# Where the first FFN's raw weights are staged, and how far ahead they are loaded, in an attention and two-FFN kernel

## The chip, the core and the metric

The kernel runs on one core of one Trainium2 chip. The metric is device time in microseconds (us) of one execution. Engines are named as in the profile: PE (TensorE matmul), PEld (its weight loads), DVE (VectorE), ACT (ScalarE), POOL (GpSimd), SP (SyncE, whose queue issues every DMA here).

## What is computed

Attention with a window of 64 positions over q, k and v of shape (4, 8, 576, 64); its output, as 2304 tokens of 512, goes through an FFN with ELU (512 to 2048 to 512), and that through an RMS norm and a gated SiLU FFN (512 to 1536 to 512).

```python
attn = softmax(where(0 <= i - j < 64, q @ k.T / sqrt(D), -1e9)); x = (attn @ v) as (2304, 512)
h = x @ w_in;  x = where(h > 0, h, exp(min(h, 0)) - 1) @ w_out
xn = x / sqrt(mean(x * x) + 1e-6) * rms_g
g = xn @ w_gate;  out = (g * sigmoid(g) * (xn @ w_val)) @ w_out2
```

All weights arrive as 64-bit floats, so the kernel reads them as pairs of 32-bit words and has to make 32-bit floats of them itself.

## The kernel before

**Stages.** The 2304 tokens run in six blocks of 384 through the first FFN (loop at L792). While block b is multiplied, the attention of block b + 1 is worked in between (`att_runs`, L269). The attention of block 0 stands alone ahead of the loop (L776 to L780). Block 0 is special: while it runs, all weights of the first FFN are converted, and they stay in SBUF for the other five blocks. From block 1 on the weights of the second FFN are prepared in the background (`prep_matrix`) and written to DRAM; the second FFN then runs from L853.

**A unit.** The first FFN's weights are 32 units of 512 columns (`w1src`, L743 to L747: in 0, in 1, out 0, in 2, out 1, ...). `Feeder` takes a unit through four stages, one unit behind the other. `load` (L317) gets a place for the 512 KB of raw words and issues the DMA (L326). `s1` takes the magnitude from the high words (ACT L333), turns the low words into their bits in place (ACT L334), clips (L336: DVE for even units, POOL for odd ones) and joins the two (DVE L338). `s2` puts in the sign (DVE L345), after which the raw words are free, gets a place for the finished unit and writes its rounded half there (L353, ACT or DVE as the planner picks). `s3` writes the remainder (POOL L359). Between these the value lies in a `wm` tile, of which there are three. `step` (L363) does `s3` of unit n - 2, `s2` of unit n - 1, `s1` of unit n, and then loads up to unit n + AHEAD - 1; three steps run before block 0 and two per hidden tile in it.

**Places.** Pool `wp` has 32 places of 4 KB per partition under one tag, `wu` (L62). Each of the 32 finished units takes one for good. Before block 0 the attention's tiles use free ones of them (`a_tile`, two half tiles to a place, 15 places in all). `tmp4` (L123) is a place of this pool for raw words or such tiles; `big4` (L293) is one of three buffers of the same size in pool `mp`, which also serve the norm (`norm_items`, L435) and the second FFN's raw words (L755). In the kernel before, raw words with an odd number, and all from 25 on, go to `big4`, the others to `tmp4`.

**Order.** The program is written in Python order, and a planner at compile time puts each engine's instructions in a fixed order from a simulated timeline; it may pull an instruction ahead of older ones that aren't ready in that timeline. Places of a tag are given out in that timeline. On the chip each engine, and SP's queue too, works its list in order: an instruction that waits holds up all behind it. PE multiplies in `mm_in` (L403) and `mm_y` (L430); between them `elu` and `split_g` run on ACT (L421, L422) and DVE (L423, L412, L413). `x_split` (L386, L387, DVE) prepares a block's input.

Of the kernel before, what the change touches and what calls it, by code (L numbers as in the profile page):

```python
# [20 lines left out]
def kernel(  # L21
# [30 lines left out]
    assert sum(BLOCKS1) == NT and H * D == DM  # L52
    PITCH0 = 1
    NSTART = 3
    AHEAD = 4
    PS0 = 12
    AHEAD2 = 6
    NS0 = 2
# [64 lines left out]
    def tmp4():  # L123

        return wp.tile([128, 1024], F32, tag="wu", name="tmp4")
# [167 lines left out]
    def big4():  # L293
        return mp.tile([128, 1024], F32, tag="big4", name="big4", bufs=3)

    def unit():
        return wp.tile([128, 2, 512], F32R, tag="wu", name="wu")

    def w_cols(w, f):

        return w.bitcast(I32)[:, f * 256:(f + 1) * 256].rearrange("(k p) f -> p k f", p=128)
# [311 lines left out]
    def prep_out(j):  # L613

        n, f, d = 4 * NP2 + j, OF[j], {}

        def first():
            fwp.load(n + 1)
            fwp.s1(n)

        def second():
            fwp.load(n + 2)
            d[0] = fwp.sign(n)

        def half(h):
            split_out(ospill[:, f, :].rearrange("p (a c) -> p a c", a=2)
                      [:, :, h * 256:(h + 1) * 256], d[0][:, h * 256:(h + 1) * 256])

        return [first, second, lambda: half(0), lambda: half(1)]
# [113 lines left out]
    w1src = [(("in", 0), w_cols(w_in, 0))]  # L743
# [12 lines left out]
    prep = [fn for t in range(2 * NP2) for fn in prep_matrix(t)]  # L756
    PREP_PER = -(-len(prep) // (len(BLOCKS1) - 2))
    prep_o = [fn for j in range(F2) for fn in prep_out(j)]
    fw1 = Feeder(w1src, lambda: big4() if fw1.loaded % 2 or fw1.loaded > 24 else tmp4(), lambda i: unit(), AHEAD, pool=True)

    n0 = BLOCKS1[0] // 128
    setup()
# [174 lines left out]
```

## Time and profile before

| | |
|---|---|
| median of three executions | 963.12 us (960.55 to 964.42) |
| the profiled execution | 966.99 us, of which the span is 965.2 us |
| PE busy | 920.6 us, 95% of the span |
| PEld busy | 866.8 us, 90% |
| DVE busy | 648.8 us, 67% |
| ACT busy | 491.5 us, 51% |
| POOL busy | 212.4 us, 22% |
| q1, the DMA queue that SP issues to | 181.96 MB, 58.1% of 16 engines' span |

Shares of the whole span are means over stages with different limits: PE is busy in nearly all of the second half, DVE in the first block. So the views below are cut to the stretch from about 20 to 144 us, in which the first FFN's weights are converted.

### The profile page before, as it was taken

The numbers are of one execution on the slowest core, as the hardware profiler recorded it, in microseconds if no ns is written. First come the engines' busy times: TensorE is split into PE (matmuls) and PEld (weight loads), VectorE is DVE, ScalarE is ACT, GpSimd is POOL, SyncE is SP. The second block draws the span as 40 slices with busy tenths as digits, with TensorE's granted clock in tenths as the row PEclk, the third lists the DMA queues.
The fourth block names the chain that finished last, engine by engine and source line by source line (L and its number), as shares of the span: only waits on it lengthen the run. The fifth ranks groups of instructions, "written<-read, shape, count | busy, mean of one in ns | idle before, by whom it ended". The sixth has DMA issues, their size and how long they took to land.

```text
span 965.2 us, 16463 instructions
## 1 busy us (share of the span) xinstructions
PE 920.6 (95%) x5916; PEld 866.8 (90%) x5916; DVE 648.8 (67%) x1449; ACT 491.5 (51%) x1201; POOL 212.4 (22%) x228
## 2 busy tenths in 40 slices
PE   6588989999999999999999999999999999999998
PEld 5487989988899899998999999899998998998996
DVE  2899998758776877776788588178363276561471
ACT  5787766665576566556545456344141442341440
POOL 2465650245245114404402100200000000000000
PEclk9699889999999999999999999999999999999999
DMA  9556530765565266546438729791984747945721
GB/s 230 165 164 193 145 110 22 203 207 162 152 197 160 92 186 187 153 107 194 162 118 276 250 69 386 278 354 48 401 327 144 280 123 246 374 136 210 235 72 66
DMA packets 150402, 183.02 MB, mean 190 GB/s; under 512 B 81712, under 2 KB 111408, under 8 KB 150320
## 3 DMA queue, kind: packets, MB, share of 16 engines
q1 hardware_dynamic: 150320, 181.96, 58.1%
q8 instruction: 47, 0.77, 0.3%
q14 instruction: 35, 0.29, 0.1%
HBM read 144.18 MB, written 37.75 MB: 188 GB/s over the span
## 4 chain that ended last, share of the span: by engine, by line
PE 63%; DVE 12%; DMA 8%; ACT 7%; POOL 4%; issue 3%; SPq 0%; POOLq 0%; DVEq 0%; ACTq 0%
PE y L691 16%; PE w L691 12%; PE y L725 10%; PE w L403 9%; PE y L430 9%; DMA pspill<-stg 5%; PE w L725 5%; DVE wm L338 3%; POOL stg L562 3%; ACT s L207 2%; DVE wm L345 2%; DVE g L412 1%; DMA big<-in_moe_w_gate_dram 1%; DVE wm L336 1%; DVE e L423 1%
## 5 line engine op out<-in xcount | busy, mean ns | idle before, releaser
L403 PE MATMUL w<-x,wu 128*128 128x384 f32 x1152 | 228.2, 346 | 17.2 <-DVE e L423 9.5
L430 PE MATMUL y<-g,wu 128*128 128x384 f32 x1152 | 223.3, 340 | 3.7 <-DVE g L412 2.5
L403 PEld LDWEIGHTS w<-x,wu 128*128 128x128 f32 x1152 | 205.7, 193 | 23.4 <-DVE e L423 11.2
L430 PEld LDWEIGHTS y<-g,wu 128*128 128x128 f32 x1152 | 201.2, 189 | 8.3 <-DVE g L412 3.9
L691 PE MATMUL y<-xw,pu 128*128 128x384 f32 x864 | 161.6, 334 | 0.0
L691 PEld LDWEIGHTS y<-xw,pu 128*128 128x128 f32 x864 | 151.2, 188 | 0.8
L562 POOL TENSOR_TENSOR stg<-wm,stg 128x256 fp32r<-128x256 f32 x72 | 64.8, 906 | 293.2 <-ACT stg L561 285.3
L691 PE MATMUL w<-xw,pu 128*128 128x384 f32 x648 | 123.7, 334 | 0.0
L657 DVE TENSOR_TENSOR c<-c,w 128x384 f32<-128x384 f32 x72 | 39.7, 551 | 118.5 <-PE w L691 117.6
L691 PEld LDWEIGHTS w<-xw,pu 128*128 128x128 f32 x648 | 113.3, 188 | 0.3
L725 PE MATMUL y<-wu,g 128*128 128x512 f32 x432 | 106.4, 390 | 0.0
L725 PEld LDWEIGHTS y<-wu,g 128*128 128x128 f32 x432 | 80.9, 188 | 16.2
L423 DVE SCALAR_TENSOR_TENSOR e<-e,w 128x384 f32<-128x384 f32 x96 | 52.5, 548 | 55.2 <-ACT e L422 54.9
L421 ACT ACTIVATE e<-w 128x384 f32<-128x384 f32 x96 | 46.3, 483 | 55.3 <-PE w L403 55.3
L653 ACT COPY c<-y 128x384 f32<-128x384 f32 x72 | 34.3, 480 | 67.9 <-PE y L691 67.3
L413 DVE TENSOR_TENSOR g<-e,g 128x384 fp32r<-128x384 f32 x96 | 62.5, 652 | 1.6
L725 PE MATMUL w<-wu,g 128*128 128x512 f32 x216 | 55.9, 390 | 0.0
L359 POOL TENSOR_TENSOR wu<-wm,wu 128x512 fp32r<-128x512 f32 x32 | 45.8, 1441 | 41.7 <-ACT wu L353 27.3
L673 ACT CAST g<-e 128x384 fp32r<-128x384 f32 x69 | 34.7, 511 | 37.2 <-DVE e L667 37.2
L207 ACT ACTIVATE s<-s,st 128x128 f32<-128x128 f32 x120 | 46.6, 390 | 10.7 <-DVE st L203 10.7
L662 ACT ACTIVATE e<-c 128x384 f32<-128x384 f32 x54 | 27.5, 524 | 47.2 <-DVE c L657 47.2
L422 ACT ACTIVATE e<-e 128x384 f32<-128x384 f32 x96 | 50.1, 524 | 1.8
(126 smaller groups left out, 1209.5 us busy)
## 6 DMA issues: line engine op xcount, KB each, us to landing
pu<-pspill SPq DMA_DIRECT2D x126, 512.0 KB, 6.5
pspill<-stg SPq DMA_DIRECT2D x84, 256.0 KB, 2.2
wu<-ospill SPq DMA_DIRECT2D x36, 512.0 KB, 5.3
big<-in_moe_w_out_dram SPq DMA_DIRECT2D x16, 512.0 KB, 4.9
big<-in_moe_w_in_dram SPq DMA_DIRECT2D x15, 512.0 KB, 3.9
vw<-in_v_dram SPq DMA_DIRECT2D x27, 256.0 KB, 3.7
tmp<-in_moe_w_out_dram SPq DMA_DIRECT2D x12, 512.0 KB, 4.7
big<-in_moe_w_gate_dram SPq DMA_DIRECT2D x12, 512.0 KB, 5.1
```

Of the source, the lines that this page charges most:

```text
L207: nc.scalar.activation(out=s[:, p, :], in_=s[:, p, :], func=AF.Exp, scale=-1.0, bias=st[:, 0, p, :], accum_out=st[:, 1, p, :])
L359: eng.tensor_tensor(out=u[:, 1, :], in0=m, in1=u[:, 0, :].bitcast(F32), op=ALU.subtract)
L403: nc.tensor.matmul(pt[:, :n], lhsT=wt[:, a, kk * 128:(kk + 1) * 128], rhs=xs[kk][:, c, :n], start=(i == 0), stop=(i == len(seq) - 1))
L413: nc.vector.tensor_tensor(out=g[:, 1, :n], in0=src[:, :n], in1=g[:, 0, :n].bitcast(F32), op=ALU.subtract)
L421: nc.scalar.activation(out=e[:, :n], in_=ph[:, :n], func=AF.Relu, scale=-1.0)
L422: nc.scalar.activation(out=e[:, :n], in_=e[:, :n], func=AF.Exp, scale=-1.0)
L423: nc.vector.scalar_tensor_tensor(out=e[:, :n], in0=e[:, :n], scalar=-1.0, in1=ph[:, :n], op0=ALU.add, op1=ALU.max)
L430: nc.tensor.matmul(py[m][:, :n], lhsT=wt[:, a, m * 128:(m + 1) * 128], rhs=g[:, c, :n], start=(first and i == 0), stop=(last and i == 2))
L562: nc.gpsimd.tensor_tensor(out=t[:, 1, :], in0=src, in1=t[:, 0, :].bitcast(F32), op=ALU.subtract)
L657: nc.vector.tensor_tensor(out=t, in0=t, in1=bank[b, qi][:, :NB], op=ALU.add)
L691: nc.tensor.matmul(bank[key][:, :NB], lhsT=u[:, qi, a, kk * 128:(kk + 1) * 128], rhs=X[j][kk][:, x, :], start=(first and n == 0), stop=(n ...
L725: nc.tensor.matmul(po[m], lhsT=g[:, a, (m % 3) * 128:(m % 3 + 1) * 128], rhs=w[:, x, :], start=(first and i == 0), stop=(last and i == 2))
```

## The change

Two lines differ. Every raw unit of the first FFN goes to a place of `wp`, and none to the three `big4` buffers; and a step loads eight units ahead instead of four. At step n there are then n finished units and the raw words of units n to n + 7, at most 24 + 8 = 32 places. Nothing that is computed changes, and no instruction is added or removed.

```diff
-    AHEAD = 4
+    AHEAD = 8
@@
-    fw1 = Feeder(w1src, lambda: big4() if fw1.loaded % 2 or fw1.loaded > 24 else tmp4(), lambda i: unit(), AHEAD, pool=True)
+    fw1 = Feeder(w1src, tmp4, lambda i: unit(), AHEAD, pool=True)
```

## Rows read from the trace of the kernel before

**Rows 1.** Busy time by stretch: start:end, length; PE, PEld, DVE, ACT, POOL; clock, DMA share, GB/s

```profile
22.00:45.00 23.00, 10.71 (x126) 8.78 (x125) 17.59 (x60) 17.99 (x54) 9.72 (x8) 0.72 0.60 165
42.00:76.00 34.00, 28.70 (x197) 27.47 (x198) 33.86 (x68) 25.61 (x59) 20.37 (x14) 0.85 0.58 178
76.00:110.00 34.00, 28.86 (x203) 26.80 (x201) 32.72 (x62) 25.23 (x59) 21.76 (x15) 0.90 0.49 149
110.00:144.00 34.00, 31.07 (x208) 28.81 (x207) 33.59 (x63) 23.08 (x55) 20.49 (x14) 0.90 0.53 139
133.00:965.00 832.00, 817.77 (x5156) 773.86 (x5155) 539.33 (x1195) 395.27 (x959) 141.50 (x161) 1.00 0.57 192
```

**Rows 2.** Chain that ended last, around 133 us: start, length, what

```profile
131.71 1.37 DVE g L412
...
133.13 1.67 PE y L430 x8
```

**Rows 3.** Waits, 38 to 144 us: engine and line, releaser, total, times, longest

```profile
ACT big L334 <- DMA big<-in_moe_w_in_dram: 2.5, 2, 1.6
DVE e L423 <- ACT e L422: 1.1, 1, 1.1
```

**Rows 4.** SP's queue in order of time, 20 to 48 us: start, length, issue

```profile
25.93 1.34 SPq L326 DMA_DIRECT2D big<-in_moe_w_in_dram  x2
27.31 1.36 SPq L326 DMA_DIRECT2D tmp<-in_moe_w_out_dram  x2
42.42 0.38 SPq L326 DMA_DIRECT2D big<-in_moe_w_in_dram  x1
...
47.36 0.61 SPq L119 DMA_DIRECT2D ks<-in_k_dram  x1
```

**Rows 5.** PE in order of time at 74.9 us

```profile
74.93 0.44 PE L164 MATMUL w<-ident,ks 128*128 128x128 f32 x2
```

**Rows 6.** DMA issues, 38 to 130 us: KB each, median us to landing

```profile
tmp<-in_moe_w_out_dram SPq DMA_DIRECT2D x9, 512.0 KB, 4.6
```

**Rows 7.** All engines in order of time, 33.9 to 38.6 us; [idle before, releaser]

```profile
34.20 0.76 DVE L353 CAST wu<-wm 128x512 fp32r<-128x512 f32 x2
34.70 3.87 POOL L359 TENSOR_TENSOR wu<-wm,wu 128x512 fp32r<-128x512 f32 x3 [12.15 <-DVE wu L353]
...
36.13 0.67 ACT L333 ACTIVATE wm<-big 128x512 f32<-128x512 f32 x1
...
37.75 0.67 ACT L333 ACTIVATE wm<-tmp 128x512 f32<-128x512 f32 x1
...
38.45 0.43 DVE L336 TENSOR_SCALAR wm<-wm 128x512 f32<-128x512 f32 x1 [3.50 <-ACT wm L333]
```

**Rows 8.** All engines in order of time at 75.2 us

```profile
75.20 1.31 POOL L359 TENSOR_TENSOR wu<-wm,wu 128x512 fp32r<-128x512 f32 x1 [1.30 <-ACT wu L353]
75.29 1.77 DVE L338 SCALAR_TENSOR_TENSOR wm<-wm,big 128x512 int32<-128x512 int32 x1
```

**Rows 9.** DVE groups by shape, 38 to 144 us: count, busy us, mean ns, idle before

```profile
L338 DVE SCALAR_TENSOR_TENSOR wm<-wm,big 128x512 int32<-128x512 int32 x18 | 18.8, 1051 | 0.0
...
L412 DVE CAST g<-e 128x384 fp32r<-128x384 f32 x15 | 11.7, 779 | 0.1
...
L338 DVE SCALAR_TENSOR_TENSOR wm<-wm,tmp 128x512 int32<-128x512 int32 x11 | 10.5, 959 | 0.2
```

**Rows 10.** Lines L338 and L412 over the whole span: ns min/median/max, first to last start

```profile
L338 DVE SCALAR_TENSOR_TENSOR wm<-wm,big x55: 677/693/1782, 22.6 to 606.0; 128x512 int32<-128x512 int32 x55
...
L412 DVE CAST g<-e x96: 342/360/1445, 57.5 to 548.6; 128x384 fp32r<-128x384 f32 x96
```

**Rows 11.** DVE groups by shape in the stretches 42:76, 76:110 and 110:144

```profile
L338 DVE SCALAR_TENSOR_TENSOR wm<-wm,big 128x512 int32<-128x512 int32 x5 | 5.1, 1026 | 0.0
...
L338 DVE SCALAR_TENSOR_TENSOR wm<-wm,big 128x512 int32<-128x512 int32 x5 | 5.7, 1141 | 0.0
...
L338 DVE SCALAR_TENSOR_TENSOR wm<-wm,big 128x512 int32<-128x512 int32 x8 | 8.7, 1094 | 0.0
```

## The prediction

> **What bounds the kernel now.** I read the table of busy time by stretch first, then the chain that ended last, then the waits of the stretch that the change touches. From 133 us on PE is the bound: it is busy 817.77 of 832 us, so 14.2 us are idle in all that follows [rows 1]. In block 0, where the first FFN's weights are converted, it is DVE: 33.86, 32.72 and 33.59 of 34 us in three equal stretches, while ACT has 8 to 11 us free in each and PE 3 to 5 [rows 1]. The chain says the same: it runs over DVE until 133.1 us and goes over to PE there [rows 2]. So block 0 ends when DVE has done its list, and a microsecond that DVE gains or loses ahead of 133 us moves the end by about one. An earlier load helps only as far as DVE stood still for want of it.
>
> **What the loads cost now.** Waits on a raw load are small: ACT stood still twice for one, 2.5 us in all [rows 3]. DVE stood still once in the stretch, 1.1 us, behind ACT's exponential [rows 3], and 3.50 us just at its start, behind ACT's L333 [rows 7].
>
> **Part 1, every raw unit in the weight pool.** It removes SP's waits for one of three big buffers. Unit 9 was issued at 42.42, far behind the four loads at 25.93 to 28.67 [rows 4]; unit 9's buffer had come free when DVE had put in the sign of unit 3. After the change the loads from 4 on can follow each other from about 26 us. Counting places by the code, there are at most 24 + 8 = 32 of 32: the last raw unit takes the place of unit 23's raw words and finished unit 24 that of its own, which the same DVE instruction frees that the rounding waits for anyway. That costs nothing; the cover is that dependency, and if a place were short the loads alone would wait, with seven units in hand.
>
> **Part 2, eight ahead.** It adds no transfer; it moves about four of 512 KB (some 2.1 MB) forward into 26 to 45 us. The engines there are 60% busy at 165 GB/s [rows 1], so 275 GB/s when busy, 7.6 us for the four, against 23 x 0.4 = 9.2 us free. Queued behind them on SP is the load of the next keys, now at 47.36 [rows 4], which PE reads at 74.93 [rows 5]: 27 us of cover, where a load takes 4.6 us [rows 6]. If that cover were gone, one late load would cost PE up to those 4.6 us. It is not: loads wait for fewer buffers than before. Three buffers lie idle for all of block 0 and are next used by the norm behind it, in the same order as before; nothing is gained there.
>
> **ACT's order.** Since L334 needs only the raw words, the planner can pull it further forward into ACT's gaps. That moves work and adds none: with 25.6 of 34 us busy [rows 1], ACT has room. The 2.5 us of waits go away, but DVE had work while ACT waited (its only idle place was the 1.1 us), so I count at most that 1.1 us.
>
> **The start.** The 3.50 us of DVE are not a load's: unit 0 is rounded at 34.20, POOL then takes three remainders in 3.87 us from 34.70, and ACT's L333 follow at 36.13 and 37.75 as the three `wm` tiles come free [rows 7]. Earlier raw words do not free a `wm` tile. Between nothing and 3.5 us I take nothing, since the rows name POOL's chain.
>
> **What POOL takes from DVE.** This is DVE's one large term that depends on the order. At 75.20 POOL starts L359, to end at 76.51; DVE's L338, started at 75.29, takes 1.77 us and ends 0.55 us behind POOL [rows 8], where the median is 693 ns [rows 10]. Over block 0 the two kinds L338 and L412 alone lose 18 x (1051 - 693) + 11 x (959 - 693) + 15 x (779 - 360) ns = 6.4 + 2.9 + 6.3 = 15.6 us so [rows 9, 10]. Both engines keep all their instructions, but a new order pairs them anew. How much that can be I take from the three stretches, which are three pairings of the same work: L338 on big buffers means 1026, 1141 and 1094 ns [rows 11], a loss of 333, 448 and 401, within 15% of their middle. So 15% of 15.6 us, 2.3 us to either side, with zero as the likeliest.
>
> The Trainium skill (SBUF — State Buffer, "Who interferes with whom") says that VectorE and GpSimd share one pair of ports as an exclusive lock, and that the order of issue decides who blocks. The trace agrees for the pair at 75.2 us. Taken to its end, the rule speaks against reading an unchanged list of instructions as an unchanged time; the rival on pairing below is that case.
>
> **The sum.** The profiled execution took 966.99 us, its span is 965.2, and 1.8 lie around it. Gain 1.1, start 0, pairing 0, blocks 1 to 5 0: 965.9. That execution stands 3.9 us above the median of 963.12; carried to the median it is **962.0 us**, which differs from before by less than the 0.5% (4.8 us) that a measurement of this kernel can tell from no change.
>
> **Rivals.**
> *Faster: the start closes up.* If the loads in hand let the planner fill DVE's 3.50 us (input split or roundings there) besides the 1.1, and pairing falls well, it is 3.5 + 1.1 + 2.3 = 6.9 us: 956 us. For it: DVE stands free there and ACT has gaps to use. Against it: the three `wm` tiles, and the input split that needs the attention's end.
>
> *Slower: the first roundings come behind more loads.* Places of one tag are given out in the program's order. Before, unit 0's place stood ahead of raw unit 4's; now it stands behind raw units 4 to 7, unit 1's behind 8, unit 2's behind 9. If the planner thereby puts the first roundings (34.20) later, the three `wm` tiles stay full longer, L333 at 36.13 and 37.75 and DVE at 38.45 come later by as much [rows 7], and DVE is full from there on. An issue took 0.67 us of SP [rows 4]; six are 4.0 us, with pairing up to 6.3: 969 us. It decides from 4.8 us on. Against it: SP had issued such loads by 28.67, before the place is wanted at 34.20 [rows 4, 7], so the chip need not wait even where the plan does.
>
> *Pairing alone.* If the order on DVE and POOL changed so much that the 15.6 us move by over 30%, the time would leave 958 to 968 on either side, 957 or 969. Three stretches within 15% speak against it.
>
> *The loads do not come earlier.* SP's queue is in order, and a place given out late could hold the raw loads where they are: 963 us. Against it: 32 places, some never used before 42 us.
>
> **How the numbers follow.** Forecast 0.50; start closes up 0.22; first roundings later 0.13; pairing 0.09 (a third each faster, slower and within); loads not earlier 0.06. Faster by over 0.5%: 0.22 + 0.03 = 0.25; slower: 0.13 + 0.03 = 0.16; within: 0.59. The range takes the bounds: 1.1 + 3.5 + 2.3 = 6.9 below 963.1 gives 956.2, 4.0 + 2.3 = 6.3 above gives 969.4; with one more microsecond on each side for the 14.2 us of PE's idle time behind 133 us, which a new order can touch, 955 to 970.5.
>
> **What the profile after would show.** Right: no L326 on SP waits for L345 before the pool is full; units 4 to 9 are issued in one run from about 26 us; no ACT wait on a raw load between 38 and 144; DVE still 96% or more busy there, with the same means of L338 and L412 within 15%; the chain goes over to PE between 131 and 135 us. Start closed: DVE's wait at 38.45 is gone and the handover is before 129. First roundings late: L353 behind 36 us, handover behind 137. What would make the prediction wrong: a handover that moves by over 5 us, or PE's idle time behind it far from 14 us.

## The result, and the profile after

The changed kernel takes 970.19 us (median of five runs, 968.09 to 972.24), the kernel before 963.49 us beside it (960.55 to 964.42): a ratio of 1.0066 with a 95% interval of 1.0048 to 1.0084. It is slower by some 6 us. The forecast was 962.0, no change; 970.19 lies just inside the slow end of the range (955 to 970.5), where the prediction had put late first roundings and pairing.

Busy time by stretch after, for [rows 1]:

```profile
22.00:45.00 23.00, 10.67 (x118) 8.49 (x119) 15.98 (x57) 20.67 (x59) 9.36 (x7) 0.66 0.89 279
42.00:76.00 34.00, 26.81 (x155) 26.06 (x156) 33.14 (x65) 25.37 (x59) 19.47 (x13) 0.80 0.39 127
76.00:110.00 34.00, 27.36 (x194) 25.20 (x193) 33.61 (x62) 24.88 (x59) 20.51 (x13) 0.90 0.57 171
110.00:144.00 34.00, 29.48 (x234) 27.13 (x233) 33.86 (x65) 21.67 (x51) 23.05 (x15) 0.90 0.27 62
133.00:965.00 832.00, 820.58 (x5158) 777.87 (x5159) 539.46 (x1195) 394.41 (x956) 144.09 (x163) 0.99 0.57 190
```

Over the three stretches DVE is as full as before (100.6 and 100.2 us), and PE behind 133 us is no less busy. What has changed is PE ahead of it: 26.81, 27.36 and 29.48 us against 28.70, 28.86 and 31.07. One row over all of block 0 shows it, first of before, then of after:

```profile
43.00:160.00 117.00, 104.62 (x723) 98.53 (x724) 113.12 (x233) 84.89 (x205) 64.30 (x42) 0.90 0.48 140
```

```profile
43.00:160.00 117.00, 99.66 (x699) 93.93 (x700) 109.63 (x212) 78.33 (x182) 64.63 (x42) 0.88 0.40 113
```

PE stood idle 12.4 us there before and 17.3 us after, and had done 24 matmul records less by 160 us. How late PE is can be read at a matmul record of a given number. In the kernel before, 965 records start ahead of the norm of block 0 (L458), the last of them at 160.24 us; in the changed kernel the 965th starts at 164.49, 4.2 us later. PE in order of time, before and after:

```profile
160.24 0.34 PE L430 MATMUL y<-g,wu 128*128 128x384 f32 x1
160.41 0.81 PE L458 MATMUL w<-big,ones 128*128 128x384 f32 x2
```

```profile
164.49 2.24 PE L430 MATMUL y<-g,wu 128*128 128x384 f32 x12
166.57 0.81 PE L458 MATMUL w<-big,ones 128*128 128x384 f32 x2
```

The chains of before and of after show where the time went:

```profile
160.58 0.65 PE w L458 x2
```

```profile
132.24 0.60 DVE s L216
...
133.43 0.75 issue
134.18 1.11 DVE s L216
...
135.42 1.09 PE w L223 x4
136.51 3.11 PE w L403 x12
...
166.73 0.65 PE w L458 x2
```

The norm is 6.2 us later, but 976 records stand ahead of it in PE's new order, 11 more than before, and these take 1.9 us. Of the 4.2 us at the 965th record, 2.3 are there when the chain goes over to PE (135.4 us, 133.1 in [rows 2]), and 2.0 come behind it, where PE has more left to do. DVE puts the sign into the last of the 32 weight units at 144.7 us instead of 143.2, 1.4 later. At the end of the span 5.3 us are lost (965.2, now 970.5), so most of the loss is there when block 0 ends. Behind it the distance at records of the same number is no constant: it lies between 1.8 and 7.0 us in the next three blocks.

Where PE waits, 43 to 166 us (line, releaser, total, times, longest), before and after:

```profile
PE w L403 <- DVE e L423: 5.6, 2, 3.9
PE w L403 <- DVE x L386: 3.3, 1, 3.3
PE w L223 <- ACT wu L353: 1.8, 1, 1.8
PE w L403 <- ACT wu L353: 1.7, 1, 1.7
...
PE w L223 <- DVE s L216: 0.6, 1, 0.6
```

```profile
PE w L403 <- DVE e L423: 6.8, 2, 4.7
PE w L403 <- DVE x L386: 5.8, 1, 5.8
PE w L223 <- DVE st L215: 5.8, 2, 3.2
PE w L223 <- DVE s L216: 2.2, 2, 1.3
PE y L430 <- DVE g L412: 1.1, 1, 1.1
```

With the small ones left out here, the waits are 15.2 us before and 21.7 after (e12 below has 20.0 and is hardly late, so this sum is no measure of the delay). The largest new one is the transposes of the next block's attention (L223), which stand in PE's queue ahead of FFN matmuls and wait for the scaling of the softmax (L214 to L216) on DVE: 0.6 us before, 8.0 after.

The loads did what the change says. SP's queue from 25 us, first and last of one run of ten raw units:

```profile
25.50 1.05 SPq L326 DMA_DIRECT2D tmp<-in_moe_w_out_dram  x1
...
33.68 0.38 SPq L326 DMA_DIRECT2D tmp<-in_moe_w_in_dram  x1
```

279 GB/s instead of 165 in that stretch, and no wait of ACT on a raw load is left between 38 and 144 us. What else is new is the order in which the planner put the work. The list of instructions is the same; 11 copies that may go to either engine changed between ACT and DVE (by the lists that e1 and e2 below hold), and on DVE, ACT, PE and POOL the sequence is another one almost from the beginning.

### The profile page after: what moved, and what is told of

The parts are those of the page before. It is cut to its first block, busy times and chain, and to the rows that moved or that the text cites. A ratio compares the mean times of both kernels' runs of the same rounds, so it can differ in the third digit from the quotient of the medians.

```text
span 970.5 us, 16477 instructions
## 1 busy us (share of the span) xinstructions
PE 917.6 (95%) x5916; PEld 865.1 (89%) x5916; DVE 649.4 (67%) x1450; ACT 491.3 (51%) x1200; POOL 213.0 (22%) x228
## 4 chain that ended last, share of the span: by engine, by line
PE 65%; DVE 10%; DMA 7%; ACT 7%; POOL 5%; issue 3%; SPq 2%; POOLq 0%; DVEq 0%; ACTq 0%
PE y L691 15%; PE w L691 12%; PE y L725 10%; PE w L403 10%; PE y L430 10%; PE w L725 5%; DMA pspill<-stg 5%; POOL stg L562 3%; DVE wm L338 3%; DVE wm L345 2%; ACT s L207 2%; SPq L119 1%; DMA big<-in_moe_w_val_dram 1%; ACT wm L333 1%; POOL sw L591 1%
## 5 line engine op out<-in xcount | busy, mean ns | idle before, releaser
L403 PE MATMUL w<-x,wu 128*128 128x384 f32 x1152 | 226.3, 345 | 16.6 <-DVE e L423 10.3
L430 PE MATMUL y<-g,wu 128*128 128x384 f32 x1152 | 223.1, 340 | 4.5 <-ACT kT L178 2.3
L403 PEld LDWEIGHTS w<-x,wu 128*128 128x128 f32 x1152 | 206.6, 194 | 20.5 <-DVE e L423 12.2
L430 PEld LDWEIGHTS y<-g,wu 128*128 128x128 f32 x1152 | 200.9, 189 | 9.2 <-issue 4.3
L691 PE MATMUL y<-xw,pu 128*128 128x384 f32 x864 | 161.6, 334 | 0.0
L423 DVE SCALAR_TENSOR_TENSOR e<-e,w 128x384 f32<-128x384 f32 x96 | 52.6, 547 | 49.7 <-ACT e L422 49.2
L413 DVE TENSOR_TENSOR g<-e,g 128x384 fp32r<-128x384 f32 x96 | 61.7, 644 | 1.8
L359 POOL TENSOR_TENSOR wu<-wm,wu 128x512 fp32r<-128x512 f32 x32 | 45.8, 1440 | 46.3 <-ACT wu L353 42.0
L422 ACT ACTIVATE e<-e 128x384 f32<-128x384 f32 x96 | 50.4, 525 | 1.9
```

What stands on the lines that cost most here:

```text
L359: eng.tensor_tensor(out=u[:, 1, :], in0=m, in1=u[:, 0, :].bitcast(F32), op=ALU.subtract)
L403: nc.tensor.matmul(pt[:, :n], lhsT=wt[:, a, kk * 128:(kk + 1) * 128], rhs=xs[kk][:, c, :n], start=(i == 0), stop=(i == len(seq) - 1))
L413: nc.vector.tensor_tensor(out=g[:, 1, :n], in0=src[:, :n], in1=g[:, 0, :n].bitcast(F32), op=ALU.subtract)
L422: nc.scalar.activation(out=e[:, :n], in_=e[:, :n], func=AF.Exp, scale=-1.0)
L423: nc.vector.scalar_tensor_tensor(out=e[:, :n], in0=e[:, :n], scalar=-1.0, in1=ph[:, :n], op0=ALU.add, op1=ALU.max)
L430: nc.tensor.matmul(py[m][:, :n], lhsT=wt[:, a, m * 128:(m + 1) * 128], rhs=g[:, c, :n], start=(first and i == 0), stop=(last and i == 2))
```

## The experiments

Each of e1 to e18 ran beside the kernel before, whose median was 963.96 to 964.63 us. "Last sign" is the start of the 32nd L345, "tail" the time from there to the start of PE's last L430 of block 0, "965th" the start of PE's 965th matmul record, "norm" that of the first L458; all four are read from the one profiled execution of each run, by order of time.

| run | us | ratio, 95% interval | last sign | tail | 965th | norm |
|---|---|---|---|---|---|---|
| before | 963.49 | 1 | 143.2 | 7.8 | 160.2 | 160.4 |
| after | 970.19 | 1.0066 (1.0048 to 1.0084) | 144.7 | 12.0 | 164.5 | 166.6 |
| e1 new places, old order | 973.95 | 1.0104 (1.0085 to 1.0123) | 143.2 | 7.8 | 160.2 | 160.4 |
| e2 new places, new order | 970.02 | 1.0067 (1.0047 to 1.0088) | 144.6 | 13.6 | 166.0 | 168.1 |
| e3 part 1 alone | 967.34 | 1.0032 (1.0020 to 1.0045) | 146.0 | 8.9 | 164.7 | 164.7 |
| e4 part 2 alone | 968.25 | 1.0043 (1.0026 to 1.0059) | 145.8 | 9.2 | 165.0 | 165.0 |
| e5 as e1, old queue behind block 0 | 966.26 | 1.0016 (1.0002 to 1.0031) | 143.9 | 8.5 | 161.6 | 161.8 |
| e6 old start, new rest | 969.02 | 1.0052 (1.0032 to 1.0072) | 143.9 | 13.5 | 165.2 | 167.3 |
| e7 new start, old rest | 964.42 | 1.0000 (0.9988 to 1.0013) | 144.5 | 8.5 | 162.2 | 162.4 |
| e8 before, g's copy on ACT | 968.49 | 1.0042 (1.0025 to 1.0058) | 143.2 | 11.7 | 162.5 | 164.6 |
| e9 as e2, scaling together | 971.48 | 1.0061 (1.0041 to 1.0081) | 147.9 | 11.1 | 166.8 | 168.9 |
| e10 before, urgent first | 976.69 | 1.0116 (1.0095 to 1.0136) | 153.5 | 9.1 | 171.8 | 172.0 |
| e11 as e2, urgent first | 976.77 | 1.0121 (1.0097 to 1.0144) | 151.6 | 11.3 | 170.7 | 172.8 |
| e12 before, scaling late | 965.58 | 1.0018 (1.0003 to 1.0033) | 144.0 | 8.0 | 161.1 | 161.3 |
| e13 as e5, new PE order | 968.77 | 1.0040 (1.0022 to 1.0058) | 143.4 | 10.4 | 161.6 | 163.7 |
| e14 as e2, old PE order | 971.56 | 1.0075 (1.0057 to 1.0094) | 148.4 | 10.0 | 167.6 | 167.7 |
| e15 before, no POOL share | 956.71 | 0.9922 (0.9905 to 0.9939) | 128.2 | 12.2 | 147.6 | 151.8 |
| e16 before, minima on DVE | 969.05 | 1.0054 (1.0035 to 1.0073) | 139.8 | 15.3 | 165.2 | 165.2 |
| e17 after, no POOL share | 956.32 | 0.9910 (0.9886 to 0.9934) | 130.2 | 11.0 | 148.7 | 152.1 |
| e18 as e15, new places | 954.15 | 0.9882 (0.9856 to 0.9908) | 130.1 | 12.3 | 149.6 | 153.7 |

Two things have to be kept apart here. The norm has no fixed place in PE's order: 964 or 965 records stand ahead of it in before, e1, e3 to e5, e7, e10, e12, e14 and e16, 976 in after, e2, e6, e8, e9, e11 and e13, and 984 to 988 in e15, e17 and e18; so PE's progress is compared at the 965th. And SP's queue behind the last raw load is that of the changed kernel in e1, e2, e6, e9, e11 and e14, and another (e5's) in e5, e7 and e13. Between e1 and e5 this queue alone moves the time by 8 us, behind block 0; so where two of these runs have different queues, their times compare more than the order.

**Loads and places, with the order held.** To change places and loads without the planner's order, or the order without them, the order is written out: each engine's instructions are chained, and the copies that may go to ACT or DVE get a fixed engine. The places are given out by hand (raw unit i and finished unit i share place i), since a pool that gives them out itself would tie the two together. In these kernels the lists stand packed; the edits below that name them (`per`, `sp`, or a row of lines) tell how a list was put together. The lines of these kernels (e1, e2, e5 to e7, e9, e11, e13, e14, e18) lie two further down, L458 being L460, and the fixed copies appear as L1148.

```diff
+    def raw_at(i): return wp.tile([128, 1024], F32, tag=wtag(i), name="tmp4")
...
-    fw1 = Feeder(w1src, tmp4, lambda i: unit(), AHEAD, pool=True)
+    fw1 = Feeder(w1src, lambda: raw_at(fw1.loaded), unit, AHEAD, pool=True)
...
+    for e in (0, 1, 2, 3):
+        seq = per[e]
+        for a, b in zip(seq, seq[1:]):
+            tc.add_manual_dep(t[b], t[a].name, mybir.DependencyInfo(
+                mybir.DependencyClass.NoSync, mybir.DependencyReason.DATA), reason="order")
```

> Both parts of the change are in: all raw words in the weight pool, eight loads ahead, and the loads on SP in the order of the changed kernel. The instructions of PE, DVE, ACT and POOL stand in the order of the kernel before, and the copies that may go to DVE or ACT are on the engine they had before. Theory (the 6.4 us come from the new order of the compute instructions): as before, 963.5 us within 2. Rival (places and earlier loads cost time themselves, through transfers that collide with the engines' work): as after, 970 us within 2. If the theory holds, DVE's wait for unit 0 near 38.5 us is again about 3.5 us and PE goes over to its own bound at 133 us.

> The same kernel with the order and the choices of engine of the changed kernel instead: places, loads and edits of the first run are all the same. Theory (order): as the changed kernel, 970 us within 2, and so 6 to 7 us above the first run. Rival (transfers): the same as the first run, whatever that is. It also shows whether writing the order out changes the time by itself; neither theory expects that.

e2 came out as the changed kernel, 970.02 us. e1 took 973.95, above both expectations. Its busy time by stretch:

```profile
22.00:45.00 23.00, 11.77 (x126) 9.72 (x125) 17.66 (x61) 17.50 (x54) 9.28 (x8) 0.74 0.90 280
42.00:76.00 34.00, 27.86 (x194) 26.35 (x195) 33.86 (x68) 25.74 (x59) 20.91 (x14) 0.85 0.43 136
76.00:110.00 34.00, 28.50 (x210) 26.37 (x208) 32.66 (x62) 25.42 (x59) 21.62 (x15) 0.95 0.60 188
110.00:144.00 34.00, 29.36 (x205) 27.10 (x205) 33.59 (x63) 23.13 (x55) 20.58 (x14) 0.95 0.24 54
```

What matters is DVE's column: 33.86, 32.66 and 33.59 us with 68, 62 and 63 instructions, where [rows 1] has 33.86, 32.72 and 33.59 with the same counts. The loads run at 280 GB/s in the first row and the places are new, and block 0 is that of before: last sign 143.2, 965th record and norm at 160.2 and 160.4. Its row over block 0:

```profile
43.00:160.00 117.00, 101.72 (x723) 95.29 (x724) 112.58 (x233) 85.19 (x204) 66.00 (x42) 0.93 0.39 113
```

PE did the same 723 records in 101.72 us at a granted clock of 0.93, where it took 104.62 at 0.90 before, stood idle 15.3 us instead of 12.4, and the norm came no later. So PE's idle time is no measure of a delay here; the records are. What e1 lost came behind block 0: at records of the same number it is level at 200 us and 9 us late at 320, 6.7 at the end. Between 200 and 300 us ACT waits for a store:

```profile
ACT stg L563 <- DMA pspill<-stg: 18.7, 11, 4.9
```

(15.0 us, longest 2.3, before.) SP's order was that of the changed kernel for the whole program there, with the compute order of another. e5 keeps it only as far as the last raw load:

```diff
-    sp = loads_of(after)
+    sp = loads_of(after)[:63] + [x for x in loads_of(before) if x not in loads_of(after)[:63]]
```

> As the first run (all raw words in the weight pool, eight loads ahead, the order of the compute instructions of the kernel before), but the order of the transfers on SP follows the changed kernel only up to the last raw load and the kernel before from there on. In the first run every engine kept within 0.1 us of the kernel before until 160 us, and lost 9 us between 200 and 300 us, where ACT waits up to 4.9 us for a store (before: up to 2.3). Theory (the change itself costs nothing; the 9 us were transfers of block 1 queued in the order of another kernel): 963.5 us within 2. Rival (the new places cost something behind block 0, when later tiles take them over): 973 again.

966.26 us, 1.5 above before by the ratio (0.2 to 3.0): most of e1's excess is gone with the queue. Places and earlier loads cost no more than that, and nothing in block 0 of e1. What remains of the loss goes with the order of the compute instructions; e14 below shows it for block 0, with all else held.

**Each part alone, the planner free.**

```diff
-    AHEAD = 8
+    AHEAD = 4
```

> Part 1 alone: every raw unit in the weight pool, loads four ahead as before; the planner orders the rest. It differs from before in 7 choices of engine. Theory (order): its time follows from an order of its own, so anything within about 7 us of 963.5, with no reason to be the same as before; if it differs, the difference is built up ahead of 135 us. Rival (the places cost): 970. Rival (the eight loads ahead cost): 963.5 within 1.

```diff
-    AHEAD = 4
+    AHEAD = 8
```

> Part 2 alone: loads eight ahead, raw units in the places of the kernel before (the three big buffers, and the weight pool for every other one up to the 24th); the planner orders the rest. Theory (order): a time of its own within about 7 us of 963.5. Rival (eight loads ahead cost): 970. Rival (the places cost): 963.5 within 1.

Both are slower, by 3.2 and 4.1 us, so neither part alone carries the whole; each has an order of its own, and so this is no sum of two costs. Read with e5, it suggests that these times come from three different orders.

**Which stretch.** The lists of the order are joined at 43 us, by the starts in the trace (e6; e7 the other way round, with e5's queue):

```diff
-    per[e] = after[e]
+    per[e] = [i for i in before[e] if start[i] < 43] + [i for i in after[e] if start[i] >= 43]
```

> New places and loads. The order and the engine choices of the kernel before for what it started ahead of 43 us, those of the changed kernel for all the rest. Theory A (the loss comes from the start: roundings that DVE did in its gap at 34 us are made on ACT there, and DVE makes others later, in its full stretch): the choices of the rest stay, so it keeps most of the loss, 968 to 971. Theory B (the loss comes from the order of the full stretch, attention's scaling and the ELU behind weight work on DVE): 969 to 971 as well. It tells them apart only together with the next run; a time near 964 would mean that the start's own order is what costs.

> The other way round: the order and engine choices of the changed kernel for what it started ahead of 43 us, those of the kernel before for all the rest. If the start costs (Theory A), 966 to 970. If only the order of the full stretch costs (Theory B), 962 to 964, and perhaps 1 us below before, since the changed kernel is 1.1 us ahead at 27 to 37 us.

969.02 and 964.42. The start of the changed kernel costs nothing in e7's time, though it leaves DVE idle longer ahead of 38.7 us; its order from 43 us on costs most of the loss (e6: 5.0 us by the ratio, of 6.4 in after). The two differ in SP's queue as well, but the 965th record says the same, 162.2 and 165.2 us. In their rows over block 0, e6 and then e7:

```profile
43.00:160.00 117.00, 98.36 (x694) 93.02 (x695) 109.06 (x207) 79.08 (x183) 65.23 (x42) 0.89 0.39 113
```

```profile
43.00:160.00 117.00, 101.50 (x712) 94.66 (x713) 111.28 (x228) 81.95 (x197) 65.75 (x42) 0.90 0.38 113
```

**Which engine's order.**

e13 starts from e5, e14 from e2:

```diff
-    per = {PE: before, DVE: before, ACT: before, POOL: before}
+    per = {PE: after, DVE: before, ACT: before, POOL: before}
```

> The fifth run (new places and loads, order of before; 966.3 us) with PE's order alone taken from the changed kernel, in which transposes and scores of the next block's attention stand elsewhere among the FFN's matmuls. DVE, ACT and POOL keep the order of before. In the runs with the new order of the stretch, PE's last matmul group of block 0 starts 12 to 13.6 us behind DVE's last sign of a weight, in those with the old order 7.8 to 8.5. If PE's own order carries that: 967 to 971 and a tail of 11 us or more. If it is the order on DVE, ACT and POOL: 964 to 967, tail as before.

> The second run (new places, loads and order; 970.0 us) with PE's order alone taken from the kernel before. If PE's own order carries the loss: 964 to 967, tail near 8 us. If it is the order on DVE, ACT and POOL: 968 to 972, tail 11 us or more.

968.77 and 971.56, with tails of 10.4 and 10.0 us, between the two forecasts. With PE's new order alone the time is 2.3 us above e5 by the ratios, whose intervals overlap, and the 965th record starts at 161.6 us in both; so a cost of PE's order is not shown. Giving PE its old order back gains nothing. e14 and e1 differ in the order of DVE, ACT and POOL, with the engine of the 11 copies, and in nothing else: places, loads, SP's queue and PE's order are the same. The 965th record starts at 160.2 us in e1 and at 167.6 in e14. So that order is enough for the delay in block 0.

**Is it attention's scaling?** My next theory was the largest new wait: transposes that wait in PE's queue for the scaling. DVE's list in e9 (L338 stands for the weight work between); e12 does the reverse to the kernel before.

```diff
-    ... L214, L338, L215, L338, L216 ...
+    ... L214, L215, L216, L338, L338 ...
```

> The second run (new places, order of the changed kernel, 970.0 us) with one edit of DVE's order: in block 0 the three instructions that scale attention's softmax (L214 to L216 in the numbering of before) stand one behind the other, where the changed kernel has weight work between them, for five groups. Nothing else moves. In that run PE stood 9.8 us in block 0 on transposes that wait for this scaling (before: 0.6). Theory (PE's in-order wait on the transposes is the loss): that wait falls to 1 to 4 us, the norm of block 0 starts near 163 instead of 168 us, and the time is 964 to 967. Rival (DVE is full, so whoever goes first, another waits as long; only DVE's sum counts): 970 again.

> The kernel before, with the second and third instruction of the scaling moved back on DVE in block 0, as far behind their exponential as the changed kernel has them (six groups, the last instruction of each by 1 to 4 us). Places, loads, the ELU and all other orders are those of before. Theory: PE waits at the transposes as in the changed kernel, 3 to 7 us in block 0 instead of 0.6; 966 to 970 us. Rival (the loss is in the ELU or the weights, not in the scaling): 964 within 1.5.

The theory found no support either way. e9 took 971.48: the transposes' wait sank only from 9.8 to 6.8 us, the ELU's rose from 7.5 to 9.5, and the last sign came 3.3 us later, at 147.9:

```profile
PE w L405 <- DVE e L425: 9.5, 4, 5.9
PE w L225 <- DVE s L218: 6.8, 3, 3.0
```

e12, with the scaling moved back in the order of before, is 0.18% above before, 1.7 us, where 2 to 6 were expected, and its 965th record is 0.9 us late. Neither run is a full test: in e12 PE waits 2.9 us for the scaling, not 8.0. But PE's waits sum to 20.0 us there (15.2 before) with hardly a delay, so a longer wait at one place need not cost as much at the end. That on a full DVE what goes first pushes back something else that PE wants fits e9, and is not shown beyond it.

**Is it what PE waits for in general?** DVE's list again, L423, L412 and L413 being the ELU and its split:

```diff
-    ... L338, L423, L345, L412, L338, L413 ...
+    ... L423, L412, L413, L338, L345, L338 ...
```

> The kernel before, all places, loads and orders as they were, with one edit of DVE's order in block 0 (50 to 152 us): what PE waits for, the ELU with its split and attention's scaling, stands right where its exponential was done in the trace of before, 1 to 4 us earlier, and the weight work makes room. DVE's work is the same. Theory (PE's idle time in block 0 is what counts, 12.4 us of it between 43 us and the norm in before): PE's waits for the ELU and the split (5.6 + 2.2 us there) shrink by 3 to 6 us; 958 to 962 us. Rival (DVE's sum bounds block 0): 964 within 1.5.

> The same edit on the changed kernel's order (the second run, 970.0 us). Theory: PE's waits for scaling (9.8 us) and the ELU (7.5 us) shrink together by 6 to 11 us; 959 to 964 us. Rival (DVE's sum): 970 within 2.

976.69 and 976.77, both far on the wrong side. In e10 DVE now stands at the head of its queue for ACT's exponential:

```profile
DVE e L423 <- ACT e L422: 7.2, 6, 1.9
```

DVE's busy time in the three stretches fell from 100.2 to 88.5 us, 11.7 less, the last sign came 10.3 us later and the 965th record 11.6. So idle time on DVE comes out at the end nearly one for one in e10; e11, with 8.1 us less than e2 (92.4 and 100.5), has its 965th record 4.7 later than e2.

**Is it DVE's list?**

```diff
-    def elu(ph, n):
+    def elu(ph, n, copy):
...
-        return split_g(e, n, nc.vector.tensor_copy)
+        return split_g(e, n, copy)
...
-            gs[f] = elu(ph, n)
+            gs[f] = elu(ph, n, nc.scalar.copy if b == 0 else nc.vector.tensor_copy)
```

> The kernel before, with one edit: in block 0 the first copy of g (the rounding ahead of the subtraction, 15 of them at 779 ns on DVE between 38 and 144 us, 11.7 us) goes to ACT. It tests the claim that DVE bounds block 0 and that a microsecond less on it is a microsecond less at the end. Theory: DVE's list is 11.7 us shorter, PE stood idle 3 to 5 us in each of the three stretches, some 12 in all, and takes over as the bound; 953 to 958 us. Rival (the order that the planner makes anew costs as much as it did in the changed kernel): 960 to 970.

968.49 us, slower, with those 15 copies gone from DVE. Of the 11.7 us only 4.2 left its busy time (95.9 for 100.2 us in the three stretches). The planner put three more roundings (L353) on DVE, which is 2.5 us of the difference. For the rest, other instructions take longer now, L345 most of all (3.5 us); L338 on big buffers went the other way (1051, now 922 ns). Three groups of DVE, 38 to 144 us, in before and then in e8:

```profile
L345 DVE SCALAR_TENSOR_TENSOR wm<-big,wm 128x512 int32<-128x512 int32 x18 | 13.6, 754 | 0.1
...
L345 DVE SCALAR_TENSOR_TENSOR wm<-tmp,wm 128x512 int32<-128x512 int32 x11 | 7.8, 712 | 0.2
...
L353 DVE CAST wu<-wm 128x512 fp32r<-128x512 f32 x3 | 1.4, 476 | 0.0
```

```profile
L345 DVE SCALAR_TENSOR_TENSOR wm<-big,wm 128x512 int32<-128x512 int32 x18 | 15.7, 874 | 0.3
...
L345 DVE SCALAR_TENSOR_TENSOR wm<-tmp,wm 128x512 int32<-128x512 int32 x11 | 9.2, 837 | 0.1
...
L353 DVE CAST wu<-wm 128x512 fp32r<-128x512 f32 x6 | 3.9, 648 | 0.0
```

L345's means rise from 754 and 712 to 874 and 837 ns. The 4.2 us became idle time: DVE waits 5.2 us in the three stretches, 4.7 of them for ACT (L422, and L412 that runs there now), where it waited 1.1 before. So the last sign is at 143.2 as before, and e8 is no test of a DVE that ends earlier. PE has a tail of 11.7 us: a new order once more.

**POOL's share.**

```diff
-            eng = nc.gpsimd if self.pool else nc.vector
+            eng = nc.vector
...
-            (nc.gpsimd if self.pool and i % 2 else nc.vector).tensor_scalar(
+            nc.vector.tensor_scalar(
```

> The kernel before with POOL's whole share of the first FFN's weights (28 subtractions L359 and 13 minima L336 between 43 and 144 us, 62.8 us on POOL) on DVE. In the trace of before DVE's instructions that run beside POOL's take 0.14 to 0.65 us more than alone (L412 995 against 342 ns, L336 1068 against 417, L413 981 against 546), about 30 us of DVE's 100 in all. DVE would get 28 x 0.72 + 13 x 0.413 = 25.6 us more and lose the 30. Theory (the stretch is POOL's doing): DVE's list is some 4 us shorter and no unit waits for POOL; 956 to 963 us. Rival (the stretch has another cause): DVE's list is 25 us longer, 980 to 990 us.

> The kernel before with only POOL's minima (L336, every other unit, 13 of 1.74 us between 43 and 144 us, 22.6 of POOL's 62.8 us) on DVE, 0.413 us each. If the stretch goes by POOL's busy time, DVE loses 30 x 22.6 / 62.8 = 10.8 us of it and gets 5.4: 5 us less on DVE, 957 to 963 us. Rival (the order that the planner makes anew decides, as in the runs with a part of the change, by 3 to 6 us): 964 to 970.

e16 makes the second edit alone. It brought the last sign forward by 3.4 us, near the 5 expected, but the time is 969.05: the tail is 15.3 us and the 965th record 4.9 late. The planner's order is new there too, which would explain it; the order was not held. e15 takes 956.71 us, faster than both kernels. Its groups on DVE, 38 to 144 us:

```profile
L359 DVE TENSOR_TENSOR wu<-wm,wu 128x512 fp32r<-128x512 f32 x29 | 20.1, 694 | 0.3 <-ACT wu L353 0.3
L338 DVE SCALAR_TENSOR_TENSOR wm<-wm,big 128x512 int32<-128x512 int32 x17 | 11.8, 695 | 0.0
...
L336 DVE TENSOR_SCALAR wm<-wm 128x512 f32<-128x512 f32 x27 | 11.6, 428 | 0.8 <-ACT wm L333 0.8
...
L412 DVE CAST g<-e 128x384 fp32r<-128x384 f32 x18 | 6.5, 362 | 0.0
```

L338 takes 695 ns and L412 362, against 1051 and 779 in [rows 9]. With POOL out of the way the stretching of these is gone, and DVE makes POOL's 42 instructions besides: the last sign comes 15.1 us earlier and PE's 965th record 12.6. The row over block 0:

```profile
43.00:160.00 117.00, 111.12 (x818) 103.86 (x818) 107.26 (x282) 87.94 (x213) 0.00 (x0) 0.97 0.46 130
```

PE is idle 5.9 us there, where it was 12.4.

**The change where loads are waited for.** In e15 ACT does stand for raw loads, 38 to 150 us:

```profile
ACT big L334 <- DMA big<-in_moe_w_in_dram: 5.3, 7, 1.7
...
ACT big L334 <- DMA big<-in_moe_w_out_dram: 1.0, 1, 1.0
```

> The changed kernel with POOL's whole share of the first FFN's weights on DVE, as run 15 did for the kernel before (956.7 us). Theory (POOL's share stretches DVE, whatever the places and loads): 950 to 960, far below the changed kernel's 970. With POOL out, run 15 has raw loads on its chain and ACT stands 7 us for them between 38 and 150 us, so loads eight ahead have something to gain for the first time; PE stands idle 5.9 us between 43 us and the norm, so no more than some 5 us: 951 to 957 if they gain, 957 to 961 if the planner's new order takes it back.

> Run 15 (the kernel before without POOL's share, 956.7 us) with all raw words in the weight pool and eight loads ahead, the order of the compute instructions and the choices of engine held as in run 15. It shows what the change is worth by itself where raw loads are waited for. Theory (ACT's 7 us of waits go, DVE and PE take over at once): 953 to 956 us. Rival (as in run 5, the earlier loads gain nothing that the end sees): 956 to 959.

956.32 us with the planner free, 954.15 with e15's order held. In e18 ACT waits for no raw load any more. By the medians the change gains 2.6 us there with the order held and 0.4 with a new one; but the intervals of e15 and e18 touch, and the profiled execution of e18 has the longer span (956.0 against 954.1), so that a gain from the change is likely at most, not shown. Both beat the kernel before by 0.9 to 1.2%.

## Why the prediction was wrong, point by point

**What bounds block 0: here it failed.** I read the chain and DVE's full rows as "block 0 ends when DVE has done its list, and a microsecond that DVE gains or loses ahead of 133 us moves the end by about one". That names one term of two. DVE's end does pass on to PE, both ways. In e10 the last sign is 10.3 us later and the 965th record 11.6; without POOL's share (e15, e17, e18) the sign is 15.1, 13.0 and 13.1 us earlier and the record 12.6, 11.6 and 10.6. But PE also loses time that DVE's end does not show. With the old lists on DVE, ACT and POOL (in e7 from 43 us on, in e10 and e12 with their edits), the record is 0.0 to 1.3 us later than the last sign explains (e1, e5, e7, e10, e12, e13). With the changed kernel's lists (in e6 from 43 us on, in e9 and e11 with their edits) it is 1.9 to 4.5 us (after, e2, e6, e9, e11, e14), and 8.3 in e16, where a last sign 3.4 us earlier ended 5 us later. In after the last sign moved by 1.4 us and the record by 4.2, and PE's tail grew from 7.8 to 12.0 us. At the last sign PE had issued 161 of block 0's 192 L430 and 181 of its 192 L403; in before it was 167 and all 192. The handover on the chain is the last place where PE waited for DVE, and says nothing of how much work PE had saved up by then. The missing row was PE's in the same window, by its records: 723 before, 699 after.

**"Both engines keep all their instructions", and the order at zero.** A new order came with the change, as I had written, and I priced it at what DVE and POOL do to each other, 2.3 us to either side. That term held, in sum. L338, L345 and L412 after, 38 to 144 us:

```profile
L338 DVE SCALAR_TENSOR_TENSOR wm<-wm,tmp 128x512 int32<-128x512 int32 x29 | 28.2, 984 | 0.2
L345 DVE SCALAR_TENSOR_TENSOR wm<-tmp,wm 128x512 int32<-128x512 int32 x28 | 24.9, 901 | 0.2
L412 DVE CAST g<-e 128x384 fp32r<-128x384 f32 x15 | 10.2, 679 | 0.2
```

L338 and L412 lose 29 x 291 + 15 x 319 ns = 13.2 us beside POOL, 2.4 less than before. L345, which the sum left out, loses more instead (901 ns, where it took 754 and 712 before). Over all kinds of DVE instruction that start between 43 and 144 us, the time above the shortest of each kind is 30.7 us before and 31.3 after, so pairing does not account for the 6 us. The step that failed is the price of the new order: I gave it pairing, and one microsecond for "PE's idle time behind 133 us", and nothing for PE ahead of that, where PE came 4.2 us late. e1 against e14, with all else the same, shows 7.4 us there from the order of DVE, ACT and POOL.

**Parts 1 and 2: right.** With the order held they cost nothing in block 0 (e1) and 1.5 us in all (e5: 0.2 to 3.0). The loads run from 25.5 us, ACT's waits are gone, and some 2.6 MB more between 22 and 45 us (280 instead of 165 GB/s) move nothing on DVE (e1). They gain nothing either, though ACT's 2.5 us of waits, 2.8 with one of 0.3 that the prediction had missed, are gone.

**The start: right, with another reason to look.** DVE's gap ahead of L336 grew from 3.50 to 5.48 us, since ACT makes all of the first three roundings, two of which DVE made before; e7 shows no cost in the time.

```profile
33.70 1.66 ACT L353 CAST wu<-wm 128x512 fp32r<-128x512 f32 x3
...
38.67 0.43 DVE L336 TENSOR_SCALAR wm<-wm 128x512 f32<-128x512 f32 x1 [5.48 <-ACT wm L333]
```

**The rivals.** The slower one gave 969 and came near the time, but not by its mechanism: the first roundings are earlier, not later (33.70, 34.20 before), and the handover is short of its 137 us. Its premise, places given out in the program's order, also disagrees with the section on the kernel before, where the planner's timeline gives them out; no run tells which. The faster one, the start closing up, did not come. The one on pairing has the right place, the order, and the wrong channel.

**The checks named.** Nearly all came out as in my forecast (one run of loads, no wait of ACT, DVE full, L338 at 984 and L412 at 679 ns, the handover within half a microsecond of 135, 11.4 us of idle time on PE behind 133 us), and the kernel was still 0.66% slower. They all looked at DVE, at the handover and behind it; none looked at PE ahead of it.

**The rule on the shared ports.** The Trainium skill (SBUF — State Buffer, "Who interferes with whom") gives VectorE and GpSimd one shared pair of ports, which one instruction holds for its whole length. e15 agrees in so far as L338, L345 and L412 take 695, 694 and 362 ns without POOL beside them, near their medians over the whole of before (693, 689 and 360). The Trainium skill (GPSIMD Engine Reference, "4.1 Engine selection") puts elementwise work on VectorE, GpSimd being about twice as slow for two inputs; L359 took 1445 ns on POOL and takes 694 on DVE. For one input the Trainium skill, in the same place, has GpSimd near the full rate; L336 took 1736 ns on POOL beside a full DVE, and never less than 1483 in the trace of before, and takes 428 on DVE; there the measurement decides. With 62.8 us of POOL's work moved back, DVE's last sign came earlier: here POOL's help cost DVE more than it saved.

**What stays open.** Which instructions of the new order hold PE back is not settled. The scaling, the largest new wait, was neither confirmed nor excluded by e9 and e12; the orders of DVE, ACT and POOL were not exchanged one by one, nor was the engine of the 11 copies taken apart from them. How the 4.2 us of block 0 become the loss at the end is not shown either, as the distance changes behind it. Nor did I show why the order of before is better than the five others that the planner made around it with POOL at work (after, e3, e4, e8, e16); that PE is later in all five is what these runs show.

## What to carry to other kernels

Where two engines are both nearly full, a chain that changes from one to the other does not name one bound: put beside it the later engine's own progress (when it starts a record of the same number; its idle time alone misled here), and price a new order by what it does to that engine's supply. An edit that only touches loads still makes the planner write a new order for everything, worth 3 to 6 us here; hold the order to see what the edit itself costs. Before an elementwise share is given to POOL, compare the durations of DVE's instructions with and without POOL beside them.

## What was unexpected in the hardware

DVE's stretched durations are not the instruction's own. Taking 15 copies of 779 ns off DVE freed 4.2 us of its busy time and not 11.7; three roundings that came to DVE are 2.5 us of the difference, and the weight work beside POOL took over much of the blocked time (L345: 754 and 712 ns, then 874 and 837). Priced at its undisturbed 342 to 362 ns, the edit was worth 5.1 to 5.4 us from the start. Also, raw loads at 280 instead of 165 GB/s beside attention's last matmuls and the first conversions left DVE's busy time in block 0 unchanged to 0.1 us (e1). And PE's idle time grew with its granted clock where nothing else changed: before and e1 have the same 723 records in block 0 and the same norm, with 12.4 us of idle time at 0.90 and 15.3 at 0.93 (means over the stretch, in which the clock is at one of two levels, 1.2 and 2.4 GHz).
